# One core's gated mix of two attentions: the output weights loaded in ten pieces, and the order of all instructions laid out anew

## The chip, the cores and the metric

The kernel runs on one core of one Trainium2 chip. The metric is the device time of one execution in microseconds (us); three executions are shown for the kernel before, and one more with a profile. TensorE (PE) multiplies matrices, ScalarE (ACT), VectorE (DVE) and GpSimd (POOL) work element by element, and SyncE (SP) issues nearly all transfers (DMAs). Each engine takes its own instructions strictly in the order in which the program lists them, and waits where the next one is not ready.

## The reference

The input x has 2048 tokens of 640 features, used by both branches, each with 32 heads of 20 features. Branch A is a linear attention with feature maps: a softmax of q and of k times a small matrix per head, with both signs. Branch B works in four segments of 512 tokens: causal softmax attention inside a segment, plus what a running memory of the segments before holds. A gate per token mixes the two.

```python
qkv = x @ wqkv                                   # A
phi_q = [softmax(q @ w_phi), softmax(-q @ w_phi)]; phi_k likewise
kv = phi_k^T v; z = sum(phi_k)
a = ((phi_q kv) / (phi_q z + 1e-6)) @ wo_A
for s in range(4):                               # B
    a_dot = softmax(q_s k_s^T * scale + mask) v_s
    a_mem = (phi(q_s) M) / (phi(q_s) z + 1e-6)
    o_s = sigmoid(beta) * a_mem + (1 - sigmoid(beta)) * a_dot
    M += phi(k_s)^T v_s; z += sum(phi(k_s))
b = o @ wo_B
g = sigmoid(x . gate_w); out = g * a + (1 - g) * b
```

## The kernel before, in words

The whole program is one list of words, ORDER, written out by hand or by a planner into the source. A loop at the end goes through the words one by one; each calls one step of one stage and so issues that step's instructions. The first two characters of a word name stage and step, and the n-th time that they appear they mean the n-th item of that stage. A digit behind them names the bank of PSUM (the memory that matmuls write) that the item uses; an "a" behind them says that ACT, and not DVE, moves the result out of PSUM. As each engine takes its instructions in this order, the list alone sets what is queued behind what. Items are counted from 0 in this text.

The stages that matter here:

- **T**: 4 transposes of x on PE; the other three quarters of the transposed x (tile xT) come by a transposing DMA, the words **L0**. **D0** loads A's query weights in the same way (into a part of the tile vA).
- **k, K, v, q** (steps 0 on PE: 5 matmuls each): keys, key features, values and queries of branch B. **k2** sends padded keys through a transposing DMA (kpads to kTs), **q2** stores queries (qd to qTp), both on SP.
- **F, W**: fold A's feature matrix into its key and query weights (fold_ps). **A** (10 matmuls, k_ps) and **B** (10, v_ps): A's keys and values, 16 chunks of 128 tokens each. **S, s, X**: sums and products of A over all tokens. **J, I, G, O**: gates and masks.
- **P**: scores of B. There are 80 items, five for each pair of head groups. P0 is PE (st_ps), P1 is the exponential on ACT (PT), P3 the causal mask on POOL. Items 0 to 2 use two tiles of two banks; from item 3 on one tile of four banks (banks4) holds all scores of an item, and there is only one such tile.
- **U** (28) and **V** (4): scores times values. U0 is PE (uv_ps), U1 an eviction (uT), U2 a transposing DMA on SP (uN), U3 to U5 are the division, on DVE and POOL. V does the same without a transfer: V0 reads the unmasked blocks and V4 the masked ones.
- **M**: the memory of B (mem_ps). **f, d, n**: A's query features (pf_ps to ET), their sums (dn_ps; d1 to d6 is a chain of six small operations on DVE) and numerators (num_ps; n2, n3 on DVE, n4 on POOL).
- **l0** sends 128 finished rows of both branches through two transposing DMAs (oT), **o0** (10 matmuls, o_ps) multiplies them by WoA and WoB, **o1** evicts and **o2** stores. For the last segment **t, b, p, a, e, z, h** do this in larger pieces.
- **R0** (second_half) gives back the memory of A's first phase and sets up the tiles of the second, WoA and WoB among them, and issues their two loads of 800 KB:

```python
        lt.WoA = wO.tile([P, KC, D], BF16, name="WoA")
        lt.WoB = wO.tile([P, KC, D], BF16, name="WoB")
        syn.dma_start(out=lt.WoA, in_=rows5(A_wo))
        syn.dma_start(out=lt.WoB, in_=rows5(B_wo))
```

Before the first word the program issues a fixed row of loads: WkB, four pieces of x, WvB, A's key weights transposed (WkT, a part of the tile phk), B's query weights, WvA and the small vectors. All instructions carry line 117 in the profile, that of the helper through which they are recorded, so the tiles tell them apart.

Of the kernel before, what the change touches and what calls it, by code (L numbers as in the profile page):

```python
# [15 lines left out]
def kernel(  # L16
# [18 lines left out]
    D = 640  # L35
    H = 32
    DH = 20
    KC = D // P
    NCH = S // P
    NSEG = 4  # L40
    L = S // NSEG
# [77 lines left out]
    ten, sca, vec, gps, syn = [Kept(e) for e in (nc.tensor, nc.scalar, nc.vector, nc.gpsimd, nc.sync)]  # L119

    def rows5(w):
        return w.rearrange("(c p) n -> p c n", p=P)
# [108 lines left out]
    lt = It()  # L231
# [170 lines left out]
    def second_half(n, step, at, ev):  # L402
        if step == 1:
            halves[1].pads()
            return
        a1.close()
        halves.append(Half(ctx.enter_context(tc.tile_pool(name="bseg1", bufs=1))))
        lt.oAp = ctx.enter_context(tc.tile_pool(name="oAp", bufs=2))
        lt.a3w = ctx.enter_context(tc.tile_pool(name="a3w", bufs=1))
        lt.bw = ctx.enter_context(tc.tile_pool(name="bw", bufs=1))  # L410
        wO = ctx.enter_context(tc.tile_pool(name="wO", bufs=1))
        lt.WoA = wO.tile([P, KC, D], BF16, name="WoA")
        lt.WoB = wO.tile([P, KC, D], BF16, name="WoB")
        syn.dma_start(out=lt.WoA, in_=rows5(A_wo))
        syn.dma_start(out=lt.WoB, in_=rows5(B_wo))

    def reorder(n, step, at, ev):
        c = 2 * n + step
# [398 lines left out]
    def tail_out(j, step, at, ev):  # L817
# [5 lines left out]
        else:  # L823
# [2 lines left out]

    STEPS = dict(w=lambda n, step, at, ev: warm_up(4, 2), T=turned, A=key, B=value, F=fold("F", WkA, WkT), W=fold("W", WqA, WqT), I=masks,
                 J=beta_gate, G=token_gate, O=both_gates, S=sums, s=blocks, X=products, Z=clear, R=second_half,
                 r=reorder, L=load_x, D=load_q, k=keys, K=key_features, v=values, q=queries, f=features,
                 d=weights, n=numerators, Y=query_features, P=scores, V=attended, U=attended_cols, M=memory, l=rows,  # L830
                 o=outputs, t=tail_A, b=tail_B, h=tail_out,
                 p=tail_first, a=tail_mid, e=tail_next, z=tail_last)
# [3 lines left out]


    ORDER = (
# [60 lines left out]

    done = {}  # L900
    for word in "".join(ORDER).split():
        i = done.get(word[:2], 0)
        done[word[:2]] = i + 1
        at = word[2:]
# [32 lines left out]
```

## Time and profile before

| what | us |
|---|---|
| three executions | 291.64, 293.09, 293.02 |
| their median | 293.02 |
| profiled execution | 292.36 |
| its span, first to last instruction | 290.6 |
| ACT busy in the span | 239.6 |
| 77 exponentials of four banks on ACT, mean of one | 1.888 |

A row of a timeline gives the start, the time, the engine, the operation and "out<-in" by tiles, how often it came in a row, and in brackets how long the engine was idle before it and what ended that. SPq is the issue of a DMA on SP: the time that SP is held, not that of the transfer. A row of waits gives the total in us, how many there were and the longest. The chain of waits follows the end of the program back from what released what. The granted clock of TensorE was 1.000 throughout.

### The profile page before, as it was taken

What the parts mean: (1) busy time and instruction counts of PE and PEld (TensorE: products, weight loads), DVE (VectorE), ACT (ScalarE), POOL (GpSimd) and SP (SyncE); (2) the same over time, 40 slices, a digit from 0 to 9 for tenths busy, and PEclk for the clock granted to TensorE, in tenths of its full rate; (3) what the DMA queues carried; (4) which work ended last, traced back from release to release, by engine and by line L of the source; (5) the groups of instructions that cost most, each with busy time, mean ns of one, the idle gap of its engine ahead of it and who ended that gap; (6) DMA issues with size and microseconds to landing.
All of it is one profiled execution on the core that took longest, in us unless ns stands there. A gap on an engine that the chain in (4) does not pass through costs nothing.

```text
span 290.6 us, 8207 instructions
## 1 busy us (share of the span) xinstructions
PE 278.1 (96%) x3233; PEld 176.2 (61%) x3233; DVE 239.8 (83%) x576; ACT 239.6 (82%) x260; POOL 183.8 (63%) x305
## 2 busy tenths in 40 slices
PE   8999999999999999999999999999999999898994
PEld 4676666667677546565546556556555555566673
DVE  5969999999699539999889988798898769989613
ACT  2478976998867899999999988999899998888801
POOL 8050000037346846797996899989789996998610
PEclk9999999999999999999999999999999999999999
DMA  7999960100110694546243425141736114356422
GB/s 226 252 237 215 166 142 11 36 2 20 20 20 20 203 158 89 72 86 134 39 92 72 106 58 104 39 106 36 124 72 139 26 41 111 83 122 126 106 62 90
DMA packets 79591, 28.10 MB, mean 97 GB/s; under 512 B 69952, under 2 KB 79552, under 8 KB 79552
## 3 DMA queue, kind: packets, MB, share of 16 engines
q1 hardware_dynamic: 78608, 26.84, 45.3%
q10 hardware_dynamic: 944, 0.74, 0.8%
q8 instruction: 25, 0.41, 0.6%
q14 instruction: 14, 0.11, 0.1%
HBM read 5.61 MB, written 2.62 MB: 28 GB/s over the span
## 4 chain that ended last, share of the span: by engine, by line
PE 66%; ACT 18%; DMA 5%; DVE 4%; POOL 3%; issue 3%; DVEq 0%; ACTq 0%; SPq 0%; POOLq 0%
ACT PT L117 15%; PE o_ps L117 9%; PE proj L117 8%; PE v_ps L117 8%; PE k_ps L117 8%; PE st_ps L117 7%; PE pf_ps L117 6%; PE q_ps L117 6%; PE uv_ps L117 4%; PE kv_ps L117 4%; DMA phk<-in_A_wqkv_dram 3%; PE mem_ps L117 2%; PE num_ps L117 2%; ACT ET L117 2%; PE zb_ps L117 1%
## 5 line engine op out<-in xcount | busy, mean ns | idle before, releaser
L117 ACT ACTIVATE PT<-st_ps 128x2048 bf16<-128x2048 f32 (+1 forms) x83 | 151.2, 1826 | 18.5 <-PE st_ps L117 14.0
L117 POOL TENSOR_SCALAR_AFFINE_SELECT PT<-PT 128x512 bf16<-128x512 bf16 (+2 forms) x116 | 80.5, 708 | 37.7 <-ACT PT L117 37.2
L117 PEld LDWEIGHTS <-xT 128*128 128x128 bf16 x640 | 59.5, 98 | 28.4 <-issue 5.7
L117 PE MATMUL st_ps<-qTp,kTs 32*128 32x384 bf16 (+3 forms) x512 | 31.8, 300 | 5.0 <-ACT PT L117 4.7
L117 ACT ACTIVATE Ek<-k_ps 128x640 bf16<-128x640 f32 x32 | 26.2, 893 | 6.2 <-PE k_ps L117 4.3
L117 POOL TENSOR_TENSOR Msb<-Msb,mtmp 128x84 f32<-128x84 f32 x24 | 9.3, 386 | 33.9 <-DVE mtmp L117 33.7
L117 DVE TENSOR_TENSOR t<-num_ps,dd 128x320 f32<-128x320 f32 x64 | 28.0, 481 | 2.3 <-POOL oA L117 1.3
L117 POOL TENSOR_TENSOR oA<-t,t 128x320 bf16<-128x320 f32 x32 | 29.1, 914 | 0.9 <-DVE t L117 0.7
L117 PEld LDWEIGHTS <-oT 128*128 128x128 bf16 x240 | 22.2, 98 | 10.4 <-issue 2.2
L117 PEld LDWEIGHTS <-kTs 32*128 32x128 bf16 (+1 forms) x552 | 14.8, 92 | 20.3 <-issue 16.3
L117 PE MATMUL proj<-WvB,xT 128*128 128x320 bf16 x160 | 26.2, 300 | 0.2 <-ACT vB L117 0.2
L117 PE MATMUL proj<-WkB,xT 128*128 128x320 bf16 x160 | 25.9, 300 | 0.0
L117 PE MATMUL q_ps<-xT,WqB 128*128 128x512 bf16 x100 | 24.9, 380 | 0.0
L117 PE MATMUL pf_ps<-xT,WqA 128*128 128x512 bf16 x100 | 24.9, 379 | 0.0
L117 PE MATMUL v_ps<-WvA,xT 128*128 128x320 bf16 (+1 forms) x160 | 24.5, 300 | 0.0
L117 PE MATMUL k_ps<-qTp,xT 128*128 128x320 bf16 x160 | 23.7, 299 | 0.1
L117 DVE TENSOR_REDUCE ksum<-Ek 128x64 f32<-128x1280 bf16 x16 | 23.3, 1455 | 0.0
L117 ACT ACTIVATE ET<-pf_ps 128x512 bf16<-128x512 f32 x40 | 22.0, 627 | 0.0
L117 POOL TENSOR_TENSOR oB<-td,tm 128x320 bf16<-128x320 f32 (+4 forms) x25 | 20.8, 835 | 0.4
L117 PE MATMUL o_ps<-WoA,oT 128*128 128x320 bf16 x120 | 20.3, 300 | 0.3 <-DVE tm L117 0.3
L117 PE MATMUL uv_ps<-PT,vB 128*32 128x512 bf16 (+1 forms) x448 | 20.4, 302 | 0.1
L117 PEld LDWEIGHTS <-phk 128*128 128x128 bf16 x370 | 17.6, 98 | 4.4 <-DMA phk<-in_A_x_dram 1.7
(115 smaller groups left out, 490.0 us busy)
## 6 DMA issues: line engine op xcount, KB each, us to landing
out_dram<-osb SPq DMA_DIRECT2D x12, 160.0 KB
qTp<-qd SPq DMA_DIRECT2D x8, 128.0 KB
WvB<-in_B_wv_dram SPq DMA_DIRECT2D x1, 800.0 KB
vA<-in_B_wq_dram SPq DMA_DIRECT2D x1, 800.0 KB
WvA<-in_A_wqkv_dram SPq DMA_DIRECT2D x1, 800.0 KB
WoA<-in_A_wo_dram SPq DMA_DIRECT2D x1, 800.0 KB
WoB<-in_B_wo_dram SPq DMA_DIRECT2D x1, 800.0 KB
qTp<-qd SPq DMA_DIRECT2D x8, 96.0 KB
```

The source lines that it names most:

```text
L117: return lambda *a, **k: kept(f(*a, **k))
```

## The change

The two loads at R0 are gone. A new word c0, ten times in the list, loads one fifth of WoA or WoB (160 KB), WoA first; five of these words stand right behind R0 and five further on, and all stand before the first o0. And ORDER is a new list of 1609 words: the same 1599 words as before beside the ten, in another order, with some other banks and some evictions given to the other engine (the k words of the start stand among the T words; D0 stands before the first L0; the J words, the small M items of the first segment, the first P and the last words stand elsewhere). No other code changes. Of the list, the start, the place of R0, the fourth d item and the end:

```diff
@@ second_half @@
         lt.WoA = wO.tile([P, KC, D], BF16, name="WoA")
         lt.WoB = wO.tile([P, KC, D], BF16, name="WoB")
-        syn.dma_start(out=lt.WoA, in_=rows5(A_wo))
-        syn.dma_start(out=lt.WoB, in_=rows5(B_wo))
+
+    def load_o(n, step, at, ev):
+        W, w = ((lt.WoA, A_wo), (lt.WoB, B_wo))[n // KC]
+        syn.dma_start(out=W[:, n % KC, :], in_=rows5(w)[:, n % KC, :])
...
@@ STEPS @@
-                 r=reorder, L=load_x, D=load_q, k=keys, K=key_features, v=values, q=queries, f=features,
+                 r=reorder, c=load_o, L=load_x, D=load_q, k=keys, K=key_features, v=values, q=queries, f=features,
...
@@ ORDER @@
-        "T00 w0 T1 T01 T02 T1 T1 T03 k00 T1 k01 k1 k02 I0 k03 k1 k00 k1 k1 K0 k01 K1 k1 K0 k02 K2 "
-        "K1 v03 k1 K2 K0 k00 k1 v1a K1 v01 k1 K2 F00 K0 L0 F01 K1 v1 v02 F1a K2 F2a v03 F1 F2 v1a "
-        "F00 v1 v00 F1a F2a F01 r0 r1 v1 v01 F1 D0 F00 F2 v02 r0 v1 F1a v03 F2a v1 r1 J4 A01 r0 "
-        "v1 J0 M00 J1 A00 A1 J2 J3 J5 A2 B01 M6 M7 A1 A3 B12 B2a A01 A2 B3 B4 A4 q03 A3 A1 k2 B00 "
-        "A2 A5 L0 B11 q1a A4 B2a A00 A3 B3a A01 A1 B4 A5 A2 A4 B02 k2 A5 A1 B13 A3 B2a A00 q2 A2 "
-        "k2 B3 q00 B4 A1 A4 L0 A3 W01 A2 B01 q1a B12 A5 W1a W2a A00 A3 B2a B3a k2 W01 A4 A1 B03 "
...
-        "s0 P3 s0 P00 X02 P1 X1 s0 k01 s0 X1 s0 U3 U03 s0 k1 U4 P3 s0 P00 U5 X00 U1 P1 s0 U2 s0 "
-        "X02 s0 X1 s0 s0 P3 P00 X1 q01 P1 R0 R1 f03 q1 U3 q2 P00 M00 P1 q02 M6 P3 O0 k2 f01 U4 K2 "
-        "M7 f1 q1 f2 P00 U5 U00 q2 f1 v02 f2 U1 P3 P1 k03 U2 v1 f01 k1 k2 K0 K1 M00 P3 f02 M6 f1 "
...
-        "M2 M6 U3 v01 U1 M7 M3 U2 M03 f1 U4 v1 P3 P00 f2 M4 f01 Y2 P1 M5 M2 o02 M6 M3 M7 M4 f1 U5 "
-        "P00 f2 o1 M00 U3 P1 f03 P3 M2 M6 M3 M5 U02 f1 P00 U4 U1 M7 f01 f2 M4 U2 P3 P1 U5 o02 M5 "
-        "f1 P00 l0 o1 P3 f2 M03 o00 M2 P1 M3 U3 M4 U4 M02 U5 o1 U01 M2 o2 M3 P00 P3 U1 Y0 d03 Y1 "
-        "U2 P1 Y2 o00 d1 M5 P3 P00 l0 M01 o1a M4 P1 d2 o00 M2 d3 M3 d4 U3 d5 U4 U5 o2 P00 o1a d6 "
-        "n02 P1 n13 P3 n00 n2 n3 n12 n2 M5 U03 n3 Y0 Y1 P00 n4 U1 o00 P1 M4 U2 P3 Y2 n4 n02 n13 "
...
-        "M2 P3 o01 Y1 P1 U5 n2 n3 l0 V02 o1a M3 M5 Y2 V4 P00 n4 V1 o03 P1 M4 V2 P3 V3 o2 n01 M5 "
-        "n10 o1 n2 P00 M02 n3 P1 n03 P3 n11 b0 M2 V00 n2 n3 M3 n4 V4 M4 Y0 Y1 P00 n4 o03 V1 P1 Y2 "
-        "P3 t0 V2 o1 Y0 V3 P3 P00 M01 Y1 P1 o02 M5 M2 Y2 o2 M3 P3 o1a P00 M4 M03 P1 V00 M2 M3 V4 "
-        "p02 V1 p11 V2 V3 P3 P00 o00 P1 M5 a0 M4 b0 o1a P3 V03 o2 V4 p00 V1 V2 V3 p01 M5 a0 b0 "
-        "p00 p13 e0 a0 e0 e0 z0 z1 z0 h0 z1 a0 h1 h0a h1 h2 h2 z0 z1 e0 h0 z0 h1 z1 h0 h2 h1a h2 ")
+        "T00 w0 T1 k01 T02 k1 T03 T1 T00 T1 k01 T1 k1 k02 I0 k03 k1 k00 k1 K0 k01 K1 k1 K0 K2 k02 "
+        "K1 k1 v03 K2 K0 k00 k1 K1 v1a v01 K2 k1 v02 v1 K0 K1 F00 v1 F01 D0 F1a K2 v03 F2a F1 F00 "
+        "F2 v00 v1 F1a F2a F01 v1 F00 F1 v01 r0 F1a F2 F2a v02 v1 r1 A01 r0 v1 A00 r0 A1 A2 v03 "
+        "A1 B00 A3 L0 v1a B11 A2 A01 B2 r1 A4 B3 B4 A00 A3 A1 B02 A5 k2 A2 B13 A4 A1 B2 L0 W01 A3 "
+        "B00 A2 B11 B3a W1a A00 A5 B2a W2a B4 A3 B3a W01 A1 B02 k2 A4 B10 A2 B4 W1 B03 L0 A4 B2a "
+        "W2 B3a B11 A5 B2a A00 B4 A3 B3a G0 A01 A1 A5 k2 A2 B4 G1 A4 B02 G2 A5 A1 B13 k2 G3 A3 "
...
+        "U4 s0 U5 U00 s0 P3 k1 P00 s0 X03 U1a s0 s0 P1 U2 s0 s0 f02 s0 X1 s0 s0 s0 M01 R0 R1 M00 "
+        "c0 M03 M6 M6 P00 c0 q01 P1 c0 U3 c0 f00 q1 c0 P3 k2 f1 K2 P00 f2 q01 M7 f1 f2 U4 f02 M6 "
+        "P3 q1 P1 q2 k03 M7 q2 v00 U5 k1 f1 M7 P00 f2 v1 U01 k2 P3 K0 K1 f03 P1 U1 K2 M00 q02 M6 "
...
+        "d3 U4 k01 d4 U5 k1 d5 q2 U00 P3 P00 c0 k1 G0 v03 U1 P1 k2 v02 d6 G1 v1 v01 G2 v1 K0 P3 "
+        "G3 P00 U2 k00 v1a P1 n03 K1 n12 O0 v01 k1 c0 n2 U00 K2 v1a P3 n3 P00 U3 c0 k03 P1 n4 U1 "
...
+        "n00 P1 n13 n3 q01 Y1 U4 n2 n4 n3 c0 U02 Y2 U5 Y0 q1 P00 c0 v00 Y0 Y1 n4 U1 l0 P1 v03 Y1 "
...
+        "M2 f01 M6 M2 P3 U2 P1 M3 M7 M3 o00 M5 f1 P3 M4 P00 l0 f2 o1 o02 U3 P1 U5 U4 M5 U00 o1 Y0 "
+        "Y1 P00 o2 P3 U1 d01 P1 U5 M4 U2 Y2 o02 d1 P3 P00 l0 M00 o1a o03 d2 P1 M5 M2 d3 M3 U3 d4 "
+        "n02 U4 n11 M4 U5 o1a d5 o2 P00 o00 P3 P1 d6 M5 n2 U03 l0 n3 o1a P3 P00 U1 n02 P1 n10 n4 "
+        "o01 n2 n3 n4 o2 n03 n12 o1 P00 Y0 P3 U2 n2 o00 P1 Y1 n3 Y2 U01 n4 o1 P00 o2 U3 P3 n03 U1 "
...
+        "o1 n12 Y0 M5 P00 M2 o2 Y1 o00 P1 P3 n2 n3 M3 V03 n4 Y2 o1a V4 P3 P00 U3 M4 l0 M02 P1 o00 "
+        "U4 V1 M2 U5 V2 M3 M5 o1 P00 P3 V3 n01 P1 o2 n10 M4 V03 n2 M5 V4 n3 n02 n11 V1 n2 Y0 P00 "
+        "V2 n4 Y1 b0 o00 P1 P3 n3 V3 n4 Y2 Y0 P00 P3 t0 o1 o02 P1 Y1 Y2 M01 o1 P3 P00 M2 M3 p03 "
+        "P1 p10 o2 M4 V02 M5 V4 Y0 Y1 P00 P3 V1 M01 P1 Y2 a0 V2 M2 V3 M3 M4 M02 P3 p00 M2 M3 V01 "
+        "M5 V4 p01 V1 V2 M4 b0 a0 V3 M5 b0 a0 e0 e0 e0 p02 p11 z0 z1 z0 h0a z1 h1 a0 h0a h1 h2 h2 "
+        "z0 z1 e0 h0a h1 z0 z1 h2 h0a h1 h2 ")
```

80 rows, old and new, of the table ORDER are left out of this document.

## The prediction

> **What bounds the kernel now.** The page comes first. TensorE (PE) is busy nearly all the time:
>
> ```profile
> span 290.6 us, 8207 instructions
> PE 278.1 (96%) x3233; PEld 176.2 (61%) x3233; DVE 239.8 (83%) x576; ACT 239.6 (82%) x260; POOL 183.8 (63%) x305
> ```
>
> By that row 12.5 us (290.6 - 278.1) would be all that a new order can win. But the end of a matmul is modelled, and its tail covers short gaps, so I read starts instead: from the first matmul of one word of the list to that of the next. All 3233 matmuls can be laid against the old list in order, so every word has its start. Most prices are read off the PE timeline and the chain:
>
> ```profile
> 121.04 0.73 PE L117 MATMUL uv_ps<-PT,vB 128*32 128x512 bf16 x16
> 121.70 0.33 PE L117 MATMUL mem_ps<-vB,phik 128*128 128x84 bf16 x4
> 122.11 0.40 PE L117 MATMUL st_ps<-qTp,kTs 32*128 32x384 bf16 x8
> 122.44 0.85 PE L117 MATMUL proj<-WvB,xT 128*128 128x320 bf16 x5
> 123.13 0.84 PE L117 MATMUL proj<-WkB,xT 128*128 128x320 bf16 x5
> ```
> ```profile
> 25.15 1.08 PE q_ps L117 x5
> 171.06 1.36 PE o_ps L117 x10
> ```
>
> From start to start: U0 0.66, P0 0.33, k0 or v0 0.68 (0.69 here); q0 and f0 1.08; o0, and A0 with as many matmuls of the same size, 1.36. The other words are priced in the same way. So, all words of a list come to 263.9 us, the same in both lists, since no PE work is added or removed. The rest of the span is start, end and waits, and that is what a list can move. Who ends PE's waits:
>
> ```profile
> PE st_ps L117 <- ACT PT L117: 4.7, 16, 0.6
> PE num_ps L117 <- DVE t L117: 1.2, 1, 1.2
> ```
>
> The first line is the loop's law. From P0 number 3 on (I count from 0), four banks hold the scores of one P0, and the next P0 must wait until ACT has read them. The chain near the end shows the bare cycle:
>
> ```profile
> 264.72 1.88 ACT PT L117
> 266.60 0.51 ACT eq L117
> 267.15 1.88 ACT PT L117
> 269.03 0.52 ACT eq L117
> 269.55 1.87 ACT PT L117
> ```
>
> 267.15 - 264.72 = 2.43 and 269.55 - 267.15 = 2.40: **no cycle from P0 to P0 is shorter than about 2.41 us**, however few matmuls lie in it. A cycle with more than 2.41 us of matmuls is bound by PE. So the list is read cycle by cycle: the larger of PE's words and 2.41. The loop's ends:
>
> ```profile
> 72.24 0.39 PE L117 MATMUL st_ps<-qTp,kTs 32*128 32x512 bf16 x4
> ...
> 273.91 0.40 PE L117 MATMUL st_ps<-qTp,kTs 32*128 32x384 bf16 x8
> ```
>
> These are P0 numbers 3 and 79. For the 76 cycles from 3 to 79 the old list's bound is 195.1 us; the trace has 273.91 - 72.24 = 201.7. The excess is 6.6 us, 0.09 a cycle, so the law holds closely and can be laid on the new list.
>
> **The change, part by part.**
>
> *Start to P0 number 3.* The old list waits for the transposed key weights:
>
> ```profile
> 12.38 0.84 PE L117 MATMUL proj<-WvB,xT 128*128 128x320 bf16 x5
> 13.73 0.81 PE L117 MATMUL fold_ps<-phk 128*128 128x140 bf16 x12 [0.51 <-DMA phk<-in_A_wqkv_dram]
> ```
>
> The word at 12.38 needs 0.68, so fold could start at 13.06 and starts at 13.73: 0.67 lost. The new list has one v0 word (0.68) more ahead of F00 and fills exactly this: -0.67. The k0 words put among the T words win nothing more, as this DMA still ends the wait. Against it, the new list has 0.66 us more words ahead of P0 number 3 (67.53 against 66.87). P0 number 0 comes later by 5.12 - 0.67 = 4.4 us, but numbers 0 to 2 then carry 8.5 us instead of 13.0. The sum to P0 number 3 is 0, so 72.2 again.
>
> In this stretch the new list also loads the query weights (D0) before the first xT piece (L0):
>
> ```profile
> 14.20 7.03 SPq L117 DMA_TRANSPOSE xT<-in_A_x_dram  x1
> 21.27 3.73 SPq L117 DMA_TRANSPOSE vA<-in_A_wqkv_dram  x1
> ...
> 27.43 2.88 PE L117 MATMUL k_ps<-qTp,xT 128*128 128x320 bf16 x20
> ```
>
> The pair leaves SP at 25.0 in either order. A0 number 4, the second half of the last line (28.79), is xT's first reader; in the new list 24.48 us of words stand ahead of it, with 4.07 before them (13.73 less the 9.66 ahead of F00), so 28.5. Landing lags an issue's end by about 1.7 us (the uN row below: 2.86 less an issue of 1.2), so 26.7 is in time. If both take 7.03, it is 28.3 + 1.7 = 29.9: late by 1.4. Bounds 0 and 1.4; I take 0, since the queue was filled ahead of the 7.03.
>
> *The loop.* The same sum over the new list, by stretch (bound; in brackets the trace):
>
> | cycles | old list | new list |
> |---|---|---|
> | 3 to 18 | 43.9 (44.9) | 42.5 |
> | 19 to 39 | 53.7 (55.6) | 54.3 |
> | 40 to 59 | 49.8 (51.4) | 49.6 |
> | 60 to 78 | 47.7 (49.8) | 47.6 |
> | all | 195.1 (201.7) | 194.1 |
>
> So **-1.0**. 47 old cycles and 50 new ones lie under the floor. Counting ACT's own words per cycle as a third limit gives 198.0 and 196.4, so -1.6; I keep -1.0.
>
> *Waits above the law.* The largest is at 246: the reciprocal chain of the fourth segment (d1 to d6) ends just before its first users, and PE stands for a num bank:
>
> ```profile
> 246.66 0.54 DVE L117 TENSOR_TENSOR dd<-rs,den 128x256 f32<-128x256 f32 x1
> ```
> ```profile
> 247.85 0.32 PE L117 MATMUL num_ps<-KV,ET 128*128 128x80 bf16 x3 [1.17 <-DVE t L117]
> ```
>
> That cycle runs 0.8 over its bound. In the new list d01 stands a step earlier, and the second n pair of that segment a cycle after d6. This may win 0.8, or the wait may turn up elsewhere: between 0 and -0.8, I take -0.5. Against it, the first U0 comes 3.09 us after its last score tile instead of 3.78: +0.2.
>
> *The ten pieces.* They take the place of two issues:
>
> ```profile
> 96.25 0.47 SPq L117 DMA_DIRECT2D WoA<-in_A_wo_dram  x1
> 96.77 0.51 SPq L117 DMA_DIRECT2D WoB<-in_B_wo_dram  x1
> ```
> ```profile
> 0.81 1.82 SPq L117 DMA_DIRECT2D phk<-in_A_x_dram  x4
> ```
>
> Pieces of the same 160 KB cost 1.82 / 4 = 0.46 of SP each, so ten cost 4.6 and the change adds 3.6 us to SP, spread over some 34 us (five right after R0, five up to cycle 24). What queues behind a piece on SP is a q2, k2, U2 or l0 word. In return no 1.6 MB stand ahead of them at once. The two lines of PE's waits above name no transfer, so there is nothing on PE to win. The last piece is issued 5.6 us of words ahead of the first o0, against one issue and 1.7. So 0 on PE; if each piece delayed the path by its issue, +3.6. I take 0, since PE's rows never name SP's transfers here.
>
> The Trainium skill (DMA: Bandwidth & Descriptors, Rules for kernel authors) speaks against this part: many small transfers should be coalesced into one large one. The two rows above agree only as far as an issue costs 0.46 whether it moves 160 or 800 KB; by the rule the time would be that of the slower rival below.
>
> *Fetches of instructions.* One wait of that look is in the old trace, and PE runs on beside it:
>
> ```profile
> ACT Ek L117 <- issue: 1.4, 1, 1.4
> ```
>
> So 0; at most -1.4.
>
> *Tail.* After P0 number 79 the old list has 12.75 us of words and takes 12.4:
>
> ```profile
> 274.31 2.82 PE o_ps L117 x20
> 277.13 1.01 PE nd_ps L117 x40
> 278.14 8.17 PE o_ps L117 x60
> ```
> ```profile
> 276.37 1.23 POOL L117 TENSOR_SCALAR_AFFINE_SELECT PT<-PT 128x512 bf16<-128x512 bf16 x2 [0.83 <-ACT PT L117]
> ```
>
> The last mask ends at 277.60, 3.69 after the P0; V4, which reads it, came at 277.58, just covered. The new list has 11.71 (-1.04), but only 3.02 of words ahead of V4: a wait of 0.67 opens. Together **-0.4**. The evictions and the last store keep their length.
>
> *Sum*: 0 - 1.0 - 0.5 + 0.2 + 0 - 0.4 = -1.7. The profiled execution took 292.36 (span 290.6 and 1.8 around it): 290.7. The median shown is 293.02, 0.7 above that execution, and its runs spread from 291.64.
>
> **Rivals.**
>
> *A wash.* The floor is the same, and the small waits come back in other cycles: the excess of 0.09 a cycle need only be 0.11 and no gain at 246 come. Then -1.7 + 0.5 + 76 x 0.02 = +0.3: 292.7. For it: DVE and POOL are at 83% and 63%, and the new list has six U steps with under 3.55 us from eviction to first use (uT's start 117.49 to 121.04, below), the old one three. Against it: of 6.6 us of excess little is such a wait.
>
> *Slower: SP's transposes reach PE.* Output rows need two of them, one after the other:
>
> ```profile
> 260.12 1.20 SPq L117 DMA_TRANSPOSE oT<-oA  x1
> 261.41 2.00 SPq L117 DMA_TRANSPOSE oT<-oB  x1
> ```
> ```profile
> 117.49 0.60 DVE uT L117
> 118.16 2.86 DMA uN<-uT
> ```
>
> Two issues of 1.2 and 1.7 to land make 4.1 if SP is free. The old list leaves at least 5.7 us of words between an l0 and its first o0, and PE never waits there. The new one leaves 4.6 to 5.3 in five of its twelve (numbers 0, 8, 10 and 11, and 9 nearly). Where SP is held 1.2 longer by another transpose, or an issue takes 2.00 as above, it decides: 5.5 against 4.6 is 0.9 late, and PE is in order. With five such places 4.5 us: -1.7 + 4.5, so 295.2. Pieces on SP, by the rule above, add to this only up to cycle 24.
>
> *Slower: xT is late* by 1.4 and the 0.8 at 246 stays: 292.4 + 0.2, within the wash.
>
> *That the pieces do nothing* is part of the forecast: the gain is all the list's.
>
> **How the numbers follow.** A run here tells about 0.5%, 1.5 us: faster is below 291.6, slower above 294.5. Forecast (290.7, itself 289 to 291.5) 0.48; wash 0.24; slower by SP or another wait of that size 0.28, high because every word of a 1600-word order moved and each engine takes its words in order, so one late word is paid by all behind it. The low end is -1.6 for the loop, -0.8 at 246, -0.4, and 1 us of today's other excess: 288.6. The high end is the slower rival, 295.2.
>
> **What would show it.** P0 number 0 near 63.5 (59.04 of words and 4.07 before them, and some small gaps), number 3 near 72.2, number 79 near 272.5; F00 still at 13.7 but with eleven k0 and v0 words before it. No idle before num_ps near 246. A wait before nd_ps in the tail. Wrong, if PE waits for oT, for xT near 28.5, or if P0 number 3 is later than 73.

## The result, and the profile after

| | before | after |
|---|---|---|
| median of 8 executions each | 292.06 | 290.76 |
| ratio, 95% interval | | 0.9945 (0.9921 to 0.9969) |
| profiled execution (its span) | 292.36 (290.6) | 290.66 (288.9) |
| P0 number 3, first of the loop | 72.24 | 72.38 |
| loop, P0 number 3 to 79 | 201.68 | 200.44 |
| P0 number 79 to the end | 16.69 | 16.11 |

The forecast was 290.7. The three parts of the span changed by +0.14, -1.24 and -0.58, together -1.7, as the forecast's sum; but this sum is made of other pieces than foreseen. The page of the changed kernel, busy times, and the loop's two ends on the PE timeline:

```profile
span 288.9 us, 8208 instructions
PE 277.0 (96%) x3214; PEld 177.4 (61%) x3233; DVE 235.9 (82%) x575; ACT 240.1 (83%) x261; POOL 183.4 (63%) x305
```
```profile
72.38 0.40 PE L117 MATMUL st_ps<-qTp,kTs 32*128 32x512 bf16 x4
...
272.83 0.40 PE L117 MATMUL st_ps<-qTp,kTs 32*128 32x384 bf16 x8
```

The share of PE's busy time is the same 96%: this number tells nothing of the change. (This profile lacks 19 of PE's 3233 records.) The loop by stretches does (us, starts of P0 to starts of P0):

| cycles | before | after | change | forecast (bound, and waits where named) |
|---|---|---|---|---|
| 3 to 18 | 44.91 | 43.58 | -1.33 | -1.4, and the wait of the first U0 +0.2 |
| 19 to 39 | 55.56 | 57.41 | +1.85 | +0.6 |
| 40 to 59 | 51.45 | 50.75 | -0.70 | -0.2 |
| 60 to 78 | 49.76 | 48.71 | -1.05 | -0.1, and the wait at 246 -0.5 |

The second stretch holds the surprise. All of PE's waits that the profile shows, in the changed kernel:

```profile
PE st_ps L117 <- ACT PT L117: 3.8, 13, 0.6
PE st_ps L117 <- DMA qTp<-qd: 1.2, 1, 1.2
PE warm_ps L117 <- DVE vA L117: 1.1, 1, 1.1
PE o_ps L117 <- ACT PT L117: 0.3, 1, 0.3
PE q_ps L117 <- issue: 0.2, 1, 0.2
```

The second line is new, and it is a transfer. On PE's timeline the four matmuls of P0 number 20, first scores of the second segment, are torn apart; on SP's timeline stands the store that the fourth needs:

```profile
118.45 0.39 PE L117 MATMUL st_ps<-qTp,kTs 32*128 32x512 bf16 x3
120.08 0.39 PE L117 MATMUL st_ps<-qTp,kTs 32*128 32x512 bf16 x1 [1.24 <-DMA qTp<-qd]
```
```profile
113.74 2.23 SPq L117 DMA_DIRECT2D qTp<-qd  x3
116.01 0.59 SPq L117 DMA_DIRECT2D WoB<-in_B_wo_dram  x1
117.11 2.18 SPq L117 DMA_TRANSPOSE kTs<-kpads  x1
119.42 1.19 SPq L117 DMA_TRANSPOSE uN<-uT  x1
```

The last store is issued by 115.97 and PE goes on at 120.08, 4.1 later. From the start of P0 number 20 to that of number 21 the cycle takes 4.38, and its words come to 2.66: 1.7 over. In the kernel before, SP and PE at the same place:

```profile
114.83 0.60 SPq L117 DMA_DIRECT2D qTp<-qd  x1
```
```profile
119.61 0.40 PE L117 MATMUL st_ps<-qTp,kTs 32*128 32x512 bf16 x4 [0.31 <-ACT PT L117]
```

There 4.2 us lay between the end of the store's issue (115.43) and its reader, and the wait named is for ACT. In the new list the store is issued about half a microsecond later, and its reader stands more than one earlier.

The place at 246, where the old list stood 1.17 for a num bank, has no wait any more. The starts of P0 numbers 68 to 70 before, and the timeline of the changed kernel at the same place:

```profile
245.70 0.40 PE L117 MATMUL st_ps<-qTp,kTs 32*128 32x512 bf16 x4 [0.28 <-ACT PT L117]
...
248.91 0.40 PE L117 MATMUL st_ps<-qTp,kTs 32*128 32x384 bf16 x8
...
251.60 0.40 PE L117 MATMUL st_ps<-qTp,kTs 32*128 32x512 bf16 x4
```
```profile
245.00 0.48 PE L117 MATMUL num_ps<-KV,ET 128*128 128x140 bf16 x6
245.53 0.40 PE L117 MATMUL st_ps<-qTp,kTs 32*128 32x512 bf16 x4
245.85 0.85 PE L117 MATMUL o_ps<-WoA,oT 128*128 128x320 bf16 x5
246.54 0.84 PE L117 MATMUL o_ps<-WoB,oT 128*128 128x320 bf16 x5
247.32 0.73 PE L117 MATMUL uv_ps<-PT,vB 128*32 128x512 bf16 x16
247.98 0.40 PE L117 MATMUL st_ps<-qTp,kTs 32*128 32x384 bf16 x8
```

Cycles 68 and 69 took 3.21 and 2.69 before and 2.45 (247.98 - 245.53) and 2.57 (number 70 starts at 250.55) after: -0.9.

### The profile page after: what moved, and what is told of

The parts are those of the page before. It is cut to its first block, busy times and chain, and to the rows that moved or that the text cites. A ratio compares the mean times of both kernels' runs of the same rounds, so it can differ in the third digit from the quotient of the medians.

```text
span 288.9 us, 8208 instructions
## 1 busy us (share of the span) xinstructions
PE 277.0 (96%) x3214; PEld 177.4 (61%) x3233; DVE 235.9 (82%) x575; ACT 240.1 (83%) x261; POOL 183.4 (63%) x305
## 4 chain that ended last, share of the span: by engine, by line
PE 70%; ACT 19%; POOL 5%; issue 2%; DMA 2%; SPq 1%; DVE 0%; DVEq 0%; ACTq 0%; POOLq 0%
ACT PT L117 16%; PE proj L117 9%; PE o_ps L117 9%; PE v_ps L117 8%; PE k_ps L117 8%; PE st_ps L117 7%; PE pf_ps L117 7%; PE q_ps L117 6%; PE uv_ps L117 4%; PE kv_ps L117 4%; POOL oA L117 2%; PE mem_ps L117 2%; POOL PT L117 2%; DMA qTp<-qd 2%; ACT eq L117 1%
## 5 line engine op out<-in xcount | busy, mean ns | idle before, releaser
L117 POOL MEMSET qTp<- 128x4096 bf16 x1 | 3.5, 3512 | 41.7 <-ACT vA L117 41.7
L117 POOL TENSOR_TENSOR oA<-t,t 128x320 bf16<-128x320 f32 x32 | 28.5, 895 | 2.1 <-DVE t L117 1.7
L117 PE MATMUL proj<-WkB,xT 128*128 128x320 bf16 x160 | 26.6, 305 | 0.0
L117 PE MATMUL q_ps<-xT,WqB 128*128 128x512 bf16 x92 | 23.5, 380 | 0.6 <-issue 0.2
L117 PE MATMUL o_ps<-WoB,oT 128*128 128x320 bf16 x120 | 20.2, 299 | 0.0
```

The costliest lines, as they stand in the source:

```text
L117: return lambda *a, **k: kept(f(*a, **k))
```

## Experiments

Times are medians in us. A ratio is to the kernel before, run on the same chip beside it, with its 95% interval. "Loop" is P0 number 3 to 79 in the profiled execution. The changed kernel itself was run once more, unedited.

> The changed kernel once more, unedited, on the chip and in the hours of the run beside it. Theory: 0.9945 of the kernel before within its interval (0.992 to 0.997), P0 number 3 to 79 in 200.4 to 200.7, P0 number 20 waiting 1.6 for qTp, and the tail 16.1. Rival (the first comparison was lucky): 0.998 or more.

Measured: 290.36, ratio 0.9948 (0.9929 to 0.9967), loop 200.79, tail 16.13. P0 number 20 waits again, a little longer (the bracket says 1.46 for 1.24). The first comparison holds. The loop is 0.1 longer than the range expected, and otherwise the profile's details repeat from execution to execution.

**Are the pieces worth anything?** Three kernels: the new list with whole loads, the old list with pieces, and the new list with one piece moved.

```diff
 lt.WoB = wO.tile(...)
+syn.dma_start(out=lt.WoA, in_=rows5(A_wo))
+syn.dma_start(out=lt.WoB, in_=rows5(B_wo))
...
-"... c0 ..."   # all ten
```

> The new list without its ten c0 words; second_half issues the two loads of 800 KB as the kernel before did. Theory (the pieces are worth nothing, the list makes the whole gain): PE does not see the loads, so 290.8 as the changed kernel, within 0.6, and P0 number 79 within 0.5 of 272.8. Rival 1 (the pieces keep 1.6 MB from standing ahead of the small transfers of queries and keys in the loop): then the whole loads at about 104 delay q2, k2 or U2, PE shows new waits for qTp, kTs or uN, and the time goes back to 292 or more. Rival 2 (ten issues cost SP 3.6 us more, which reaches PE through the late qTp at 118): then it is faster than the changed kernel, 289.3 to 290.

Measured: 290.53, 0.9965 (0.9945 to 0.9985); loop 200.73; P0 number 20 stands 1.5 as in the changed kernel. The intervals of this and of the changed kernel (around 0.9945 and 0.9948) overlap for more than half of their length.

```diff
-"... P1 R0 R1 f03 q1 U3 q2 P00 M00 ..."
+"... P1 R0 c0 R1 f03 c0 q1 c0 U3 c0 q2 P00 c0 M00 ..."   # and five more, each behind a P00
```

> The old list with ten c0 words put in (five behind R0, five up to P0 number 25) in place of the two loads, nothing else. Theory (pieces worth nothing): 292.1 as the kernel before, within 0.6. Rival 1 (the pieces make the gain): 290.8. Rival 2 (many small transfers in place of large ones cost the path their issue): up to +3.6, so 293 to 295.7.

Measured: 291.56 beside 291.61, 0.9998 (0.9980 to 1.0016); loop 201.36. The pieces neither win nor cost anything that these runs can tell, to about 0.2% either way: not by the 3.6 us of SP that the forecast estimated, and not by the bytes ahead of other transfers.

```diff
-"U00 P3 P00 c0 k1 G0 v03 U1 P1 k2 ... P3 G3 P00 U2 k00"
+"U00 P3 P00 k1 G0 v03 U1 P1 k2 ... P3 G3 P00 U2 c0 k00"
```

> The changed kernel with one piece of the output weights (c0 number 5, issued at 116.0, just behind the last store into qTp) put behind the next two transposes on SP. Theory (the store is late by its place in the list): the wait inside P0 number 20 stays, 1.2 to 1.6, and the time stays at 290.8 within 0.5. Rival (the piece's 160 KB get in the way of the store's landing): the wait shrinks to 0.5 or less and the time falls by about 1, to 289.8.

Measured: 290.44, 0.9964 (0.9943 to 0.9984); cycle 20 still 1.67 over its words. So the late store isn't late because of the piece issued behind it. In this kernel, in the changed one and in the one with whole loads the fourth matmul of P0 number 20 starts 4.0 to 4.1 after the end of that issue (4.05, 4.12, 4.02), whatever is issued next. What makes up these 4 us, no run here shows.

**Is the law of the cycle right?** It says that nothing is won in a cycle with fewer than 2.41 us of words and all above it in the others. Matmuls were left out of the one and of the other.

```diff
-for X, Wo in ...: for k5 in range(KC): ten.matmul(... m == 0 ... m == 2 * KC - 1)
+left = [(X, k5) ...][::2 if n in (5, 7, 8, 9, 12, 15, 17, 21, 22, 23) else 1]
+for X, k5 in left: ten.matmul(...)
```

> The changed kernel with 5 of the 10 matmuls left out (every second one) in ten o0 items that stand in cycles of at most 2.41 us of words: numbers 5, 7, 8, 9, 12, 15, 17, 21, 22, 23. That is 6.8 us of PE work gone, and part of those ten output blocks isn't computed. Theory (no cycle is shorter than 2.41): P0 number 3 to 79 stays within 0.5 of 200.5 and the time within 0.5 of the changed kernel. Rival (PE at 96% busy is the bound): -6.8.

Measured: loop **200.45 against 200.44**: 6.8 us of matmuls gone and not a hundredth of it won. Each of the ten cycles kept its length to 0.01. Cycle 68, shown above for the changed kernel, with half of its o0 left out:

```profile
244.85 0.40 PE L117 MATMUL st_ps<-qTp,kTs 32*128 32x512 bf16 x4
245.18 0.58 PE L117 MATMUL o_ps<-WoA,oT 128*128 128x320 bf16 x3
245.60 0.43 PE L117 MATMUL o_ps<-WoB,oT 128*128 128x320 bf16 x2
245.97 0.56 PE L117 MATMUL uv_ps<-PT,vB 128*32 128x512 bf16 x8
246.85 0.35 PE L117 MATMUL uv_ps<-PT,vB 128*32 128x256 bf16 x8 [0.33 <-POOL PT L117]
247.30 0.40 PE L117 MATMUL st_ps<-qTp,kTs 32*128 32x384 bf16 x8
```

247.30 - 244.85 = 2.45, the same. PE just waits elsewhere. The median, though, was 291.86, 0.9993 (0.9978 to 1.0008): by the ratios some 1.3 us above the changed kernel, where at most 0.5 was expected. The profiled execution, 290.69, is the fastest of the ten; its tail is 0.7 longer than the changed kernel's, and PE waits there for the last transposed output rows (0.54 by the profile). Why most executions took longer still stays open, as only one was profiled.

```diff
+# o0 numbers 1, 3, 6, 11, 13, 20 with every second matmul; of f0
+last = KC - {8: 3, 13: 2, 14: 2, 16: 2, 17: 2}.get(n, 0)
```

> The changed kernel with about the same amount left out in cycles of more than 2.41 us of words: 5 of 10 matmuls in o0 numbers 1, 3, 6, 11, 13, 20, 3 of 5 in f0 number 8 and 2 of 5 in f0 numbers 13, 14, 16, 17. That is 6.45 us of PE work gone (so many products of output blocks and of A's query features aren't computed). Theory (a cycle costs the larger of its words and 2.41): each falls to the floor and no further, together -3.9, so 3 to 79 in 196.6 and the time about 3.9 below the changed kernel. Rival 1 (PE busy is the bound): -6.45. Rival 2 (another engine holds the loop): 0 to -1.5.

Measured: 290.59, 0.9970 (0.9957 to 0.9984); loop 199.74, **-0.7, not -3.9**. The time is no lower than the changed kernel's, as the tail is 0.6 longer (16.72; PE waits 0.84 there for transposed rows of A). The law failed here, and cycle by cycle it is plain where. In cycles 51, 66 and 73 ACT has little to do: they fell from 2.77, 2.80 and 2.80 to 2.44, 2.44 and 2.46, to the floor as expected. The other eight did not. In seven of them stand exponentials of A's query features on ACT, two for each f item; in the eighth, cycle 39, an eviction and an exponential of queries. ACT's timeline, first of the changed kernel, then of this one with 2 of 5 matmuls of f0 left out in these cycles:

```profile
224.67 1.88 ACT L117 ACTIVATE PT<-st_ps 128x2048 bf16<-128x2048 f32 x1
226.44 1.08 ACT L117 ACTIVATE ET<-pf_ps 128x512 bf16<-128x512 f32 x2
227.40 1.90 ACT L117 ACTIVATE PT<-st_ps 128x2048 bf16<-128x2048 f32 x1
229.15 1.12 ACT L117 ACTIVATE ET<-pf_ps 128x512 bf16<-128x512 f32 x2
230.11 1.94 ACT L117 ACTIVATE PT<-st_ps 128x2048 bf16<-128x2048 f32 x1
```
```profile
223.94 1.88 ACT L117 ACTIVATE PT<-st_ps 128x2048 bf16<-128x2048 f32 x1
225.72 1.08 ACT L117 ACTIVATE ET<-pf_ps 128x512 bf16<-128x512 f32 x2
226.67 1.90 ACT L117 ACTIVATE PT<-st_ps 128x2048 bf16<-128x2048 f32 x1
228.43 1.12 ACT L117 ACTIVATE ET<-pf_ps 128x512 bf16<-128x512 f32 x2
229.38 1.93 ACT L117 ACTIVATE PT<-st_ps 128x2048 bf16<-128x2048 f32 x1
```

ACT goes without a gap in both, and one exponential follows the other after 2.73 and 2.71 in both. These cycles have **two** limits near 2.75, PE's words and ACT's, and taking the one away shows the other. With ACT's words as a third limit (the larger of PE's words, 2.41, and ACT's words) the bound goes from 196.4 to 195.4, -1.0, for the -0.7 measured. This sum is an estimate, and it fits better than its parts. Part of what an f cycle lost came back in the next one (cycle 30 -0.46, cycle 31 +0.26; cycle 49 -0.12, cycle 50 +0.29), as ACT's backlog went on into it, which a sum cycle by cycle doesn't hold. And the 0.36 won in cycle 66 came back whole in cycle 68, where PE now waits for a result of DVE.

**Can the late store be mended?** Four attempts bring the last two query projections of the second segment forward.

```diff
-"f2 k03 P1 U2 M7 k02 k1 P3 d01 k1 k2 K0 K1 P3 P00 d1 q00 P1 q03 K2 U3 q1a d2 P3 P00 q1 q2 k02 P1 ..."
+"f2 q03 P1 U2 M7 q02 q1a P3 d01 q1 q2 q2 P3 P00 d1 k00 P1 k03 U3 k1 d2 P3 P00 k1 k2 K0 K1 k02 P1 ..."
```

> The changed kernel with the last two query projections of segment 1 (q0 numbers 8 and 9 with their evictions and stores) two cycles earlier, and the keys k0 numbers 12 to 15 behind them in their places. Theory (PE stands 1.2 to 1.6 us inside P0 number 20 because the last store into qTp is issued 4 us ahead of it and lands too late): the wait for qTp goes and nothing else is late, so 289.2 to 289.8 against 290.8. Rival (another transfer is as late: k2 number 7 leaves SP at the same time as before and P0 number 21 reads its keys): the wait turns up 2.7 us later before P0 number 21, and the time stays at 290.4 to 290.8.

Measured: 290.25, 0.9954 (0.9938 to 0.9969); loop 200.21. The wait for qTp is gone, as forecast, and 19 to 39 fell from 57.41 to 55.80. But 3 to 18 grew from 43.58 to 44.96: d0 and two queries stand in one cycle (bound +0.7), and the exponential of P0 number 18 stood behind K0, which waited for keys (0.75). So 1.4 of the 1.6 us won came back in the cycles ahead. Neither the theory nor the rival came true, since the loss turned up earlier and not later.

```diff
-"... d01 q1 q2 q2 P3 P00 d1 k00 P1 k03 U3 k1 d2 P3 P00 k1 k2 K0 K1 k02 P1 d3 K2 ..."   # q_first
+"... q1 q2 q2 P3 P00 d01 k00 P1 k03 U3 d1 k1 k1 d2 P3 P00 P1 k2 K0 K1 k02 d3 K2 ..."
```

> The changed kernel with the query projections q0 numbers 8 and 9 two cycles earlier as in the run before (q_first), but with the two things mended that this run lost by: d0 number 0 goes a cycle later, so that cycles 16 to 18 hold 2.49, 2.77 and 2.35 of PE words (bound 194.1 as in the changed kernel, and not 194.8), and the exponentials of P0 numbers 18 stand ahead of K0 on ACT. Theory (law of the cycles and the late store add up): no wait for qTp, P0 number 3 to 79 in 198.6 to 199.0 against 200.4 to 200.7, and the time 1.5 lower than the changed kernel, 288.9 to 289.5 beside 291.6 of the kernel before. Rival (the stretch is held by something else, such as DVE's chain d1 to d6 or the keys for P0 number 21): 3 to 79 stays above 199.8.

Measured: 291.45, 0.9984 (0.9966 to 1.0001); loop 200.83. The rival came true. k0 number 15 took the bank that d0 still held (0.61 waiting for DVE), and three later words of PE waited for DVE, 0.24 to 0.52 each.

```diff
-"P00 d01 k00 P1 k03 U3 d1 k1 k1 d2 P3 P00 P1 k2 K0 K1 k02 d3 K2 U4 k01 d4 U5 k1 d5 U00 P3 P00 c0 k1 G0 v03 U1 ..."
+"P00 k00 P1 k03 U3 k1 d01 k1 k2 K0 K1 d1 P3 P00 k02 P1 U4 k03 k1 U5 k1 k2 d2 U00 P3 P00 c0 U1 G0 v03 d3 d4 ..."
```

> As q_first_even (query projections q0 numbers 8 and 9 two cycles earlier, d0 number 0 a cycle later), with what held that run mended: k0 number 15 no longer shares d0's bank, so it needn't wait for d1 and d2, the key evictions and the two v evictions stand ahead of K2, d5 and d6 on DVE, and k2 number 7 ahead of the piece on SP. Theory (the wait for qTp is 1.6 to 1.7, and DVE's order was what kept the gain): P0 number 3 to 79 in 198.7 to 199.4 against 200.4 to 200.7, the time 1 to 1.7 below the changed kernel. Rival (DVE or the stores just cannot be earlier here): 3 to 79 at 200 or more, the time that of the changed kernel.

Measured: 291.10, 0.9966 (0.9949 to 0.9982); loop 201.07. Cycles 3 to 18 are at 43.72 and the wait for qTp is gone, but cycles 19 and 20 lose 0.6 and 1.2 to key evictions that are late on DVE.

```diff
-"k1 k2 K0 K1 d1 P3 ... v02 v1 v1 K2 d5 v01 d6 G1 G2 K0 P3 G3 P00 U2 k00 v1a P1 n03 K1 n12 O0 v01 k1 c0 n2 ..."
+"k1 k2 K0 d1 P3 ... v02 v1 v1 d5 v01 d6 K0 P3 P00 U2 k00 v1a P1 n03 k1 K2 K1 n12 G1 G2 v01 c0 n2 G3 O0 ..."
```

> As q_first_banks, with DVE's order mended at the two places where that run gave its gain back (0.55 and 1.16 us of waiting for key evictions behind d1 and behind the gates): d1 goes ahead of K1, and the eviction of k0 number 16 ahead of K1, K2 and the gates G1 to G3 and O0. Theory (each of these waits was one late word on DVE, and behind them nothing else is late): cycles 19 and 20 at 2.5 and 2.75, P0 number 3 to 79 in 198.8 to 199.5, the time 1 to 1.5 below the changed kernel, 289 to 289.5. Rival (DVE itself is full here, so that its backlog only shows in the next word): 3 to 79 at 200 or more, the time that of the changed kernel or above.

Measured: 290.42, 0.9950 (0.9931 to 0.9969); loop 200.35. Those two waits shrank, and a new one of 0.68 for DVE came one cycle further. The rival came true again. The busy time of the engines between 113.6 and 126, in this kernel, in the changed one and in the one before:

```profile
113.60:126.00 12.40, 11.52 (x129) 6.86 (x128) 12.18 (x28) 10.20 (x11) 6.21 (x11) 1.00 0.66 110
```
```profile
113.60:126.00 12.40, 11.16 (x123) 6.42 (x121) 9.80 (x26) 9.76 (x11) 6.81 (x12) 1.00 0.58 105
```
```profile
113.60:126.00 12.40, 11.77 (x138) 7.29 (x137) 12.20 (x33) 12.20 (x13) 9.59 (x17) 1.00 0.54 79
```

The columns are stretch, length, and busy time of PE, weight loads, DVE, ACT and POOL, with the number of instructions in brackets. Without the wait DVE is busy 12.18 of 12.40 us; with it 9.80. The edits moved some of DVE's work too, so the three rows don't hold the same work. But in the changed kernel DVE goes without a gap to speak of from 113.61 to 119.29, and 1.99 of the 2.6 us in which it stands idle come in one piece behind that, ended by PE, which itself stood still until 120.08:

```profile
121.28 0.49 DVE L117 CAST kpads<-proj 128x320 bf16<-128x320 f32 x1 [1.99 <-PE proj L117]
```

So the wait for the store is the visible end of a stretch in which DVE has no room: take it away, and in three of the four attempts DVE's backlog ends the next wait. P0 number 3 to 40 says the same: 100.47 before, 100.99 changed, 100.76, 101.32, 101.09 and 100.85 in the four attempts. No order tried here beats the changed kernel beyond the intervals.

**Would moving the chain d1 to d6 alone win what the new list won at 246?** On the old list, twice.

```diff
-"f2 M03 o00 M2 P1 M3 ... U01 M2 o2 M3 P00 P3 U1 Y0 d03 Y1 U2 P1 Y2 o00 d1 M5 P3 P00 l0 M01 ... d2 o00 M2 d3 ..."
+"f2 M03 d03 M2 P1 M3 ... U01 M2 M3 P00 P3 U1 d1 Y0 o00 Y1 U2 P1 Y2 o1 o2 d2 o00 M5 d3 P3 P00 l0 d4 M01 ... d5 o00 M2 ..."
```

> The old list and the two whole loads, with the fourth segment's sums d0 and the chain d1 to d6 about a cycle earlier (d0 number 3 changes places with an o0; the bound of the list stays at 195.1). Theory (the wait for a num bank at 246 costs its cycle 0.8 and the next 0.3): no idle before num_ps there and cycles 68 and 69 at 2.41 each, so -0.8 to -1.1, 290.5 to 290.8. Rival (the wait turns up elsewhere, in the rows of DVE or in the o1 and M items that the chain now stands ahead of): 0 to -0.3.

Measured: 296.06, 1.0154 (1.0138 to 1.0170). d0 shares bank 3 with the M item ahead of it, and the second o0 bank 0 with the first:

```profile
239.18 1.16 PE L117 MATMUL dn_ps<-HZ,ET 128*128 128x16 bf16 x40 [1.49 <-DVE tm L117]
...
244.93 1.19 PE L117 MATMUL o_ps<-WoA,oT 128*128 128x320 bf16 x5 [1.98 <-DVE osb L117]
```

Two clashes of banks cost 4.3 us: this is the size of the forecast's slower rival, by another mechanism.

```diff
+"f2 M00 d03 ... U1 d1 Y0 o01 Y1 U2 P1 Y2 o1 o2 d2 o00 ..."   # banks put right, else as above
```

> The old list with the fourth segment's d0 and its chain d1 to d6 a cycle earlier as in d_earlier_old, but with the banks put right: the M item ahead of d0 uses bank 0, so d0 doesn't wait for its eviction, and the two o0 items behind it use banks 1 and 0. Theory (the wait at 246 costs 0.8 in its cycle and 0.3 in the next, and the 4.9 that the first try lost came from the shared banks alone): P0 number 60 to 79 in 48.7 to 49.2 against 49.75, the time 0.5 to 1 below the kernel before. Rival (there is no place a cycle earlier that doesn't make something else wait): 49.7 or more.

Measured: 292.11, 1.0003 (0.9987 to 1.0018); 60 to 79 in 50.29 against 49.76. The wait for the num bank shrank from 1.17 to 0.46, but cycle 66 became 0.57 longer than its words (PE waits for the eviction of uT) and cycle 68 is still 0.63 over the floor. The rival came true: the chain's place alone doesn't win it. The new list has also moved what stands around it; which of these moves took the wait away was not tested by itself.

## Why the prediction was right, point by point

- **The time and the sum** (290.7, -1.7): right, with compensating errors inside. That they compensate so closely is luck: a store that the forecast didn't look at cost 1.7, and the rest of the loop fell by about 1.6 more than it had foreseen (-2.9 for -1.3).
- **Start to P0 number 3** (0): +0.14 in the profiled executions, +0.4 as a mean over all profiles (71.7 in four with the old list, 72.1 in ten with the new). The step that failed is "0.67 lost" at F00: that wait belongs to one execution. The transposing load took 7.12 of SP there and 6.00 in the old list with pieces, where F00 doesn't wait:

```profile
4.59 6.00 SPq L117 DMA_TRANSPOSE phk<-in_A_wqkv_dram  x1
```
```profile
12.51 0.84 PE L117 MATMUL proj<-WvB,xT 128*128 128x320 bf16 x5
13.18 0.79 PE L117 MATMUL fold_ps<-phk 128*128 128x140 bf16 x12
```

  Three of four old profiles have no such wait, so a term read from one execution was taken for a property of the kernel. In the changed kernel F00 waits for nothing, and still starts later than the forecast's 13.7:

```profile
13.99 0.73 PE L117 MATMUL fold_ps<-phk 128*128 128x140 bf16 x11
```

  The forecast also said that the k0 words among the T words win nothing more; they cost. Over the ten profiles of the new list the k0 word there takes 0.69 to 1.33 from start to start, 0.34 on the mean over its 0.68, and F00 starts 0.33 later on the mean than with the old list (13.76 against 13.43). This fits the +0.4; no run moves that word alone. The last section shows what slows it. The xT load (0) was right: A0 number 4 starts at 29.00 without a wait.
- **The loop's bound** (-1.0): the floor is shown to 0.01 by leaving work out of floored cycles. The law was incomplete: ACT's words are a limit too, as the cycles with f words show. With ACT's words counted from one P0 of the list to the next, the bound moves by -1.6 (198.0 to 196.4; by stretch -1.0, -0.1, -0.3, -0.1), the number that the forecast worked out and set aside. This too is an estimate, as it lets no backlog of ACT go from one cycle into the next; whether -1.0 or -1.6 is nearer, no run shows. By it, what the stretches changed beyond the bound is waits: +1.9 in 19 to 39, -0.3 to -1.0 in the others.
- **Waits above the law** (-0.5 and +0.2): -0.9 at 246, a little more than the bound of 0.8, as the next cycle gained as well; no wait for the first U0 is in the list of waits. The missing step is the store into qTp, +1.7. The forecast checked transfers that the diff names (oT, xT, the pieces) and the distance of U steps, not that of q2 to its first reader, so it saw no new wait in 19 to 39.
- **Pieces** (0): right, by both exchanges. The Trainium skill's rule (DMA: Bandwidth & Descriptors, Rules for kernel authors) that small transfers be coalesced would have made this the slower rival; at 160 KB a piece, the measurement is 0.9998.
- **Fetches of instructions** (0): ACT's 1.4 us at the start is no longer in the changed kernel's list of waits, and nothing followed from it. What that gap was, no run shows.
- **Tail** (-0.4): -0.6. The change in words (-1.04) stands; the wait that it opens was mis-sized. The forecast put 3.02 us of words ahead of V4. By the rows they are about 3.4 (P0 0.33, two M items 0.15 each, a large A item 1.36, the large output item below 0.81, V0 0.61), so the wait foreseen there would be about 0.3 and not 0.67. And the wait opens earlier than foreseen, at that output item, which needs the four banks of the last P0, and is 0.27:

```profile
275.26 0.97 PE L117 MATMUL o_ps<-WoB,kTs 128*128 128x320 bf16 x6 [0.27 <-ACT PT L117]
276.07 1.16 PE L117 MATMUL nd_ps<-vB,PT 128*128 128x32 bf16 x40
```

  That item holds PE for 0.81, so V4 behind it finds its masks done.
- **Rivals**: oT never ends a wait of PE. The wash was half true: as much time as was won at 246, and more, was lost at P0 number 20, in a stretch where DVE is full.

## What to carry to other kernels

Where a list goes round in cycles, price each cycle by every engine that must finish in it, not by the busiest alone: two limits of nearly the same size hide each other, and leaving work out of one shows the other. A wait at the end of a full stretch is often only where the backlog becomes visible; look at the busy time of the other engines in that stretch before mending it. And take a wait that a transfer ends from several executions, since a load that took 7.1 us in one took 6.0 in the next.

## What was not expected of the hardware

PE's first microseconds run at about half speed, though the profile's granted clock reads 1.00 there, and how many differs from execution to execution. The k word that now stands among the transposes, in the changed kernel and in the one with the piece moved:

```profile
4.65 1.49 PE L117 MATMUL proj<-WkB,xT 128*128 128x320 bf16 x5
5.93 1.23 PE L117 MATMUL tp_ps<-ident,phk 128*128 128x128 bf16 x15
```
```profile
4.62 0.97 PE L117 MATMUL proj<-WkB,xT 128*128 128x320 bf16 x5
5.43 1.00 PE L117 MATMUL tp_ps<-ident,phk 128*128 128x128 bf16 x15
```

From start to start 1.28 and 0.81 for the same five matmuls, against 0.68 later in the span: moved into the first 6 us, a word costs up to 0.6 more. The Trainium skill (TensorE: Matmul & The Clock Gate, What's actually happening) has PE at half clock until it was busy for about 3.4 us, in windows that don't start with the kernel, so that the change comes at another time in each run. The runs agree with the kind, and the time is longer here: PE's first matmul was at 1.06, and in the changed kernel the slow rate still held through the word that ended at 5.93, 4.9 later.
